# Three token blocks of 768 in place of four of 512 and a rest of 256, with the seven-product up for all of them

## The chip, the cores and the metric

The kernel runs on one core of one Trainium2 chip. The metric is the device time of one execution in microseconds. The profile is of one execution, taken by the hardware profiler; its span runs from the first instruction to the last. Engines: PE is TensorE's matmul stream, PEld its weight loads, DVE is VectorE, ACT ScalarE, POOL GpSimd, SP SyncE, whose queue issues the transfers.

## The reference

Three stages follow each other on 4 x 576 = 2304 tokens. The tokens are tiled by 128 into 18 tiles.

```python
# Performer attention: q, k, v [4, 8, 576, 64], omega [128, 64]
def phi(x):
    proj = np.einsum('bhsd,md->bhsm', x, omega)
    h = proj - np.sum(x * x, axis=-1, keepdims=True) / 2.0
    return np.exp(h - np.max(h, axis=-1, keepdims=True)) / np.sqrt(m)
kv = np.einsum('bhsm,bhsd->bhmd', phi(k_s), v)
num = np.einsum('bhsm,bhmd->bhsd', phi(q_s), kv)       # divided by phi(q) . sum of phi(k)
# dense mixture: x [2304, 512], w1 [8, 512, 1024], w2 [8, 1024, 512]
P = np.exp(x @ w_gate - max)                            # then 8 Sinkhorn steps
for e in range(8):
    out += P[:, e:e + 1] * (np.maximum(x @ w1[e], 0.0) @ w2[e])
# last layer: w_in [512, 2048], w_out [2048, 512], given as float64
h = x @ w_in
out = (h * (1.0 / (1.0 + np.exp(-1.702 * h)))) @ w_out
```

## The kernel before

**Precision.** Each large product runs as float32r passes over exact splits (hi, lo): hi*hi + hi*lo + lo*hi, so each takes three matmuls where one would do. ACT makes hi by a cast, DVE or POOL makes lo by a subtraction.

**Chunks, blocks and visits.** The two layers with hidden columns are cut into chunks of 256 of them: 4 for each of 8 experts and 8 for the last layer, 40 in all. The tokens are four blocks of 512 (one for each batch) and a rest block of 256. A visit is one chunk with one block: an up product, h^T = act(w1^T x^T), and a down product, which adds the chunk's share of y to an accumulator in SBUF (`down`, L877: 6 matmuls of 128x512 for a tile of 128 tokens; the eviction L884 multiplies by the gate and adds; L888 only adds). The up product of a visit is issued ahead of the down product of the visit before it. In expert 0 the visits run block by block while attention gives blocks out, and the chunk order zigzags; from expert 1 on every chunk visits all blocks.

**Two forms of up.** `up` (matmul L714) is the ordinary product. `up_fast` (`prod`, matmul L818) is Winograd's form with seven products of quadrants (half of the chunk's columns, half of the block's tokens), each 6 matmuls of 256 columns. It accumulates in two halves of one PSUM bank `pa` (`le` and `ri`) and in `pc`. The copies L835 and L842 (ACT) and the additions L838, L843 and L847 (DVE) combine them; L689 and L697 make h's hi and lo. It is used for the four blocks of 512 in all chunks but expert 0's, the first of expert 1, called (1,0), and the first of the last layer. The rest block and the other chunks take `up`.

**Weave.** `weave` puts the four down tiles of the visit before between the parts of a fast up: one after the three first products, one after the next two, two after the sixth, and the seventh product last. A visit after the rest block has only two such tiles: none, one, one.

**Weights.** A chunk's w1 is a raw tile from one transfer, split into a pair with two buffers; the sums of quadrants that the fast form takes are made on POOL (L642) and split into another pair (L581). w2 has two rows of 128, each a pair with three buffers. `prepare` says in which visit each is made. The sums of x^T (`x_sums`) are made once for a block.

**Attention and filling.** `attention` steps through the tiles of k and q of each batch. TensorE's work in a query step is `num` (L294), a transpose of x (L342), of the next tile (L202), of features (L287) and the projection `pj` (L227 to L229). After each yield the loop at L1089 takes as much of the mixture's visits as the step's own estimate, once a block of x^T is in `ready`. All general PSUM tiles share one ring of six banks (`ps`). During experts 1 to 7 a background task turns the float64 weights into float32 in 64 pieces (L544 to L566) through a scratch in DRAM.

The order of instructions on each engine is that in which the program issues them (a manual schedule); the generators `moe`, `weave`, `up`, `up_fast`, `down` and the loop at L1089 set it.

## Time and profile before

| | |
|---|---|
| median of 3 runs | 2146.57 us (2145.16 to 2147.8) |
| span of the profiled execution | 2144.3 us |
| PE busy | 2118.2 us, 99%, 13150 matmuls |
| PEld | 1890.2 us, 88% |
| DVE | 1372.2 us, 64% |
| ACT | 741.5 us, 35% |
| POOL | 465.7 us, 22% |

The profiled execution's span is 2.3 us under the median of the timed runs. Matmuls are pipelined: the duration of one (0.28 us at 256 columns) overlaps the next, so the pace is read from the distance between starts. The idle time in a row is that of its engine just before the instruction, with what ended it.

### The profile page before, as it was taken

How to read it: one execution, taken by the hardware profiler on the slowest of the kernel's cores; microseconds unless marked ns; L12 is line 12 of the kernel's file. 1: busy time of each engine (PE TensorE's matmuls, PEld its weight loads, DVE VectorE, ACT ScalarE, POOL GpSimd, SP SyncE). 2: the span in 40 equal slices, each digit the busy share in tenths (PEclk: the TensorE clock that was granted, in tenths of full speed). 3: DMA queues.
4: the chain of work that ended last, by engine and by line, in shares of the span. 5: the costliest groups of instructions: out<-in, count | busy, mean ns of one | idle time of the engine just before them, and what ended most of it. 6: DMA issues, size and time to landing. Idle time of an engine off the chain costs nothing.

```text
span 2144.3 us, 32561 instructions
## 1 busy us (share of the span) xinstructions
PE 2118.2 (99%) x13150; PEld 1890.2 (88%) x13150; DVE 1372.2 (64%) x2625; ACT 741.5 (35%) x1628; POOL 465.7 (22%) x444
## 2 busy tenths in 40 slices
PE   8999999999999999999999999999999999999999
PEld 8888878888989999989899899998998988898888
DVE  7666556676666666666666666666555566655565
ACT  6655442432222222222222222222222245333333
POOL 3222011342211112122111111221111135222320
PEclk9999999999999999999999999999999999999999
DMA  8242111101111111111111111111000000000002
GB/s 184 51 105 58 40 40 40 50 26 45 43 57 42 57 45 50 43 45 43 57 42 49 54 46 47 45 43 52 21 27 23 21 20 21 20 21 20 20 20 89
DMA packets 113383, 97.60 MB, mean 46 GB/s; under 512 B 61008, under 2 KB 90192, under 8 KB 113232
## 3 DMA queue, kind: packets, MB, share of 16 engines
q1 hardware_dynamic: 113232, 95.52, 15.3%
q8 instruction: 103, 1.69, 0.3%
q14 instruction: 48, 0.39, 0.1%
HBM read 82.40 MB, written 13.11 MB: 45 GB/s over the span
## 4 chain that ended last, share of the span: by engine, by line
PE 93%; DVE 4%; ACT 2%; issue 1%; DMA 1%; POOL 0%; SPq 0%; ACTq 0%; DVEq 0%
PE py L877 44%; PE pa L818 27%; PE ph L714 11%; PE pc L818 4%; PE num L294 1%; PE kv L264 1%; DVE w2l L581 1%; PE pj L227 1%; PE pj L229 1%; PE pj L228 1%; DVE mx L231 1%; PE pt L202 1%; ACT feat L247 0%; PE qt L287 0%; DMA r<-in_moe_w_dram 0%
## 5 line engine op out<-in xcount | busy, mean ns | idle before, releaser
L877 PE MATMUL py<-w2h,hh 128*128 128x512 f32 x1440 | 568.6, 395 | 1.7 <-DVE xl L346 0.8
L877 PE MATMUL py<-w2l,hh 128*128 128x512 f32 x1440 | 563.5, 391 | 3.4 <-DVE w2l L581 3.4
L877 PE MATMUL py<-w2h,hl 128*128 128x512 f32 x1440 | 563.2, 391 | 0.6 <-DVE hl L695 0.6
L884 DVE SCALAR_TENSOR_TENSOR a<-py,pg,a 128x512 f32<-128x512 f32 x504 | 374.9, 749 | 162.2 <-PE py L877 153.1
L877 PEld LDWEIGHTS py<-w2h,hl 128*128 128x128 f32 x1440 | 270.3, 188 | 62.1 <-DVE hl L695 1.0
L877 PEld LDWEIGHTS py<-w2l,hh 128*128 128x128 f32 x1440 | 270.7, 188 | 45.9 <-DVE w2l L581 4.7
L877 PEld LDWEIGHTS py<-w2h,hh 128*128 128x128 f32 x1440 | 271.1, 188 | 44.8 <-DVE xl L346 1.0
L818 PE MATMUL pa<-th,w1h 128*128 128x256 f32 x816 | 233.6, 286 | 1.2 <-ACT c L835 0.8
L835 ACT COPY c<-pa 128x512 f32<-128x512 f32 x136 | 79.9, 588 | 444.5 <-PE pa L818 439.5
L818 PE MATMUL pa<-th,w1l 128*128 128x256 f32 x816 | 230.3, 282 | 0.0
L818 PE MATMUL pa<-tl,w1h 128*128 128x256 f32 x816 | 229.0, 281 | 0.0
L566 POOL TENSOR_TENSOR tmp<-tmp 128x256 f32<-128x256 f32 x64 | 47.2, 738 | 777.1 <-DVE tmp L563 409.3
L818 PE MATMUL pa<-xh,w1h 128*128 128x256 f32 x648 | 182.3, 281 | 0.0
L818 PE MATMUL pa<-xh,w1l 128*128 128x256 f32 x648 | 182.2, 281 | 0.0
L818 PE MATMUL pa<-xl,w1h 128*128 128x256 f32 x648 | 181.9, 281 | 0.0
L818 PEld LDWEIGHTS pa<-th,w1h 128*128 128x128 f32 x816 | 153.2, 188 | 18.4 <-ACT c L835 7.3
L689 ACT ACTIVATE hh<-c 128x512 fp32r<-128x512 f32 x216 | 113.5, 526 | 158.0 <-DVE c L847 115.1
L818 PEld LDWEIGHTS pa<-th,w1l 128*128 128x128 f32 x816 | 153.5, 188 | 9.2
L842 ACT COPY c<-pa 128x256 f32<-128x256 f32 x136 | 50.8, 373 | 316.2 <-PE pa L818 316.2
L818 PEld LDWEIGHTS pa<-tl,w1h 128*128 128x128 f32 x816 | 155.5, 191 | 0.0
L843 DVE TENSOR_TENSOR c<-pa,c 128x256 f32<-128x256 f32 x136 | 57.8, 425 | 149.4 <-ACT c L842 149.4
L697 DVE SCALAR_TENSOR_TENSOR hl<-c,hh 128x512 fp32r<-128x512 f32 x216 | 148.2, 686 | 0.0
(183 smaller groups left out, 4137.0 us busy)
## 6 DMA issues: line engine op xcount, KB each, us to landing
r<-in_moe_w_dram SPq DMA_DIRECT2D x82, 512.0 KB, 3.7
raw<-in_moe_w_in_dram SPq DMA_DIRECT2D x32, 256.0 KB, 3.2
raw<-in_moe_w_out_dram SPq DMA_DIRECT2D x32, 256.0 KB, 3.2
k<-in_k_dram SPq DMA_DIRECT2D x16, 256.0 KB, 4.6
v<-in_v_dram SPq DMA_DIRECT2D x16, 256.0 KB, 5.4
q<-in_q_dram SPq DMA_DIRECT2D x16, 256.0 KB, 4.6
scr_in<-tmp SPq DMA_DIRECT2D x32, 128.0 KB, 2.0
scr_out<-tmp SPq DMA_DIRECT2D x32, 128.0 KB, 1.8
```

Source lines behind the costliest of these rows:

```text
L202: nc.tensor.transpose(pt[:, i * P : (i + 1) * P], x[:, 2 * i : 2 * i + 2, :], ident)
L227: nc.tensor.matmul(o, hi[:, p, :], om_hi, start=True, stop=False)
L566: nc.gpsimd.tensor_tensor(out=mf, in0=mf, in1=af, op=ALU.add)
L689: nc.scalar.activation(self.hi, self.src, AF.Relu)
L697: nc.vector.scalar_tensor_tensor(out=self.lo, in0=self.src, scalar=0.0, in1=h, op0=ALU.max, op1=ALU.subtract)
L714: nc.tensor.matmul(ph[:, :n], a[:, kk, fs], x[:, kk, :], start=m == 0, stop=m == 3 * NK - 1)
L818: nc.tensor.matmul(o, a[kk][x], b[kk][y], start=start and kk == 0 and n == 0, stop=kk == 1 and n == 2, skip_group_check=True,)
L835: nc.scalar.copy(s[:, 0:3:2, :], pa.rearrange("p (c n) -> p c n", c=2))
L842: nc.scalar.copy(s[:, 1, :], le)
L843: nc.vector.tensor_tensor(out=s[:, 1, :], in0=ri, in1=s[:, 1, :], op=ALU.add)
L877: nc.tensor.matmul(py, a[:, f, c], w, start=m == 0, stop=m == 3 * NF - 1)
L884: nc.vector.scalar_tensor_tensor(out=o, in0=py, scalar=pg[:, i, e : e + 1], in1=o, op0=ALU.mult, op1=ALU.add)
```

## The change

The tokens become three blocks of six tiles, 768 tokens. `ORDER` places the two tiles that hold the last 64 rows of two batches each behind batches 0 and 1, and behind batches 2 and 3. A quadrant of a block has 384 columns (`Q`). `up_fast` (matmul L817) runs for every block of 35 chunks, all but expert 0's and the first of the last layer; `up` (L705) computes the same quadrants one after the other, 12 matmuls of 384 each. `le` has its own bank twice, `ri` one; the ring `ps` falls from six banks to five. h is kept in quadrants of 384, five buffers for hi and five for lo. The down product is L887, its evictions L894 and L898.

The fast up's parts hold one down tile after the third product, one after the fifth, one after the sixth, and the rest after the seventh.

w1's seven quadrants and sums stand in one raw tile, loaded by four transfers. They are split in three groups (`g0`, `g1`, `g2`) with one buffer each, made new behind the last product of the old chunk that reads the group. w2 is a ring of five tiles: the first hi is made in the middle of a chunk's first visit, the other three (L637, L639) once the last down tile of the chunk before is issued. In attention the inputs are loaded tile by tile, eight steps ahead; logits are taken for half a block; only block 0 is given out before attention ends, and the loop takes 0.65 of the step's estimate.

```diff
     NITER = 8
+    ORDER = [0, 1, 2, 3, 4, 5, 6, 7, 16, 8, 9, 10, 11, 12, 13, 14, 15, 17]
+    PLACE = {i: n for n, i in enumerate(ORDER)}
+    ST = 6
+    NB = NTILE // ST
+    SUP = ST * P
+    Q = SUP // 2
...
-        return ph["sb"].tile(shape, dt, tag="f4", bufs=5, name=name)
+        return ph["sb"].tile(shape, dt, tag="f4", bufs=4, name=name)
 
     def b2(shape, dt, name):
-        return ph["sb"].tile(shape, dt, tag="b2", bufs=15, name=name)
-    def c3(shape, dt, name):
-        return ph["sb"].tile(shape, dt, tag="c3", bufs=1, name=name)
+        return ph["sb"].tile(shape, dt, tag="b2", bufs=26, name=name)
...
+    def sx(name):
+        return big.tile([P, Q], F32, tag="sx", bufs=3, name=name)
...
-        return pp.tile([P, 512], F32, tag="ps", bufs=6, name=name)
+        return pp.tile([P, 512], F32, tag="ps", bufs=5, name=name)
...
+                j, t = divmod(PLACE[token_tile(*seq[s - 3][1:])], ST)
+                if t % 3 == 2:
+                    got = j, t // 3, logits(j, t // 3)
+                    yield 1.39
+                    if t == ST - 1 and j == 0:
+                        ready.add(j)
...
+            if 1 <= s < n - 8:
+                load_tile(*seq[s + 8])
+            if 4 <= s and at(s + 5, "k"):
+                load_tile("v", *seq[s + 5][1:])
...
-    def split_single(r, hi, lo, eng):
+    def split(r, hi, lo, eng):
         nc.scalar.copy(hi, r)
         eng.tensor_tensor(out=lo, in0=r, in1=hi.bitcast(F32), op=ALU.subtract)
 
     class Chunk:
-        """Weights of one chunk as (hi, lo): w1, sums of its quadrants where the up product is the
-        fast one, and w2 in rows of 128."""
+        GROUPS = ((0, 3), (3, 5), (5, 7))
+        SLOT = {(0, 0): 0, (0, 1): 2, (1, 1): 4, (1, 0): 5}
+        T1, T2, T3, T4 = 1, 3, 5, 6
...
-            self.r1 = big.tile([P, NK, FC], F32, tag="r1", name="r1")
-            nc.sync.dma_start(out=self.r1, in_=src)
+            self.raw = big.tile([P, 7, 2, P], F32, tag="w", name="w")
+            for (f, kh), o in self.SLOT.items():
+                nc.sync.dma_start(
+                    out=self.raw[:, o], in_=src[:, 2 * kh : 2 * kh + 2, f * P : (f + 1) * P]
+                )
...
+        def make_sums(self):
+            if self.summed:
+                return
+            self.summed = True
+            r = self.raw
+            for o, x, y in ((1, 5, 0), (3, 4, 1), (5, 4, 5), (6, 2, 3)):
+                nc.gpsimd.tensor_tensor(out=r[:, o], in0=r[:, x], in1=r[:, y], op=ALU.subtract)
+        def split1(self, i, eng):
+            a, b = self.GROUPS[i]
+            pair = [
+                big.tile([P, b - a, 2, P], F32R, tag=f"g{i}{x}", name=f"g{i}{x}") for x in "hl"
             ]
...
+            self.g[i] = pair
+            u = slice(0, b - a) if self.fast else (slice(0, 3, 2), slice(1, 2), slice(0, 1))[i]
+            split(self.raw[:, a:b][:, u], *(x[:, u] for x in pair), eng)
...
+        def split2(self, part):
+            def new():
+                return big.tile([P, DM], F32R, tag="w2", bufs=5, name="w2")
             if part == 0:
...
+                hi = new()
+                nc.scalar.copy(hi, self.r2[:, 0, :])
+                self.w2.append([hi])
+                return
+            for f in range(NF):
+                if f:
+                    self.w2.append([new()])
+                    nc.scalar.copy(self.w2[f][0], self.r2[:, f, :])
+                lo = new()
+                nc.vector.tensor_tensor(
+                    out=lo, in0=self.r2[:, f, :], in1=self.w2[f][0].bitcast(F32), op=ALU.subtract
+                )
+                self.w2[f].append(lo)
...
+    def new_h():
+        return [big.tile([P, Q], F32R, tag=f"h{x}", bufs=5, name=f"h{x}") for x in "hl"]
...
+        le = ph["ps"].tile([P, 512], F32, tag="le", bufs=2, name="le")[:, :Q]
+        ri = ph["ps"].tile([P, 512], F32, tag="ri", name="ri")[:, :Q]
+        pc = ps("pc")[:, :Q]
+        prod(le, 0, b00, True)
         run_late()
...
+        m1 = sx("m1")
+        nc.scalar.copy(m1, le)
+        prod(ri, cur.T1, s1, True)
+        m5 = sx("m5")
+        nc.scalar.copy(m5, ri)
+        prod(pc, 2, b10, True)
+        add(pc, pc, m1)
+        prep("g0")
+        yield 18 * 0.1735
+        yield next(dn)
+        steps(act(0, 0, pc))
+        prod(le, cur.T2, s2, False)
+        u2 = sx("u2")
+        nc.scalar.copy(u2, le)
+        prod(ri, 4, s4, False)
+        add(ri, ri, u2)
+        prep("g1")
+        yield 12 * 0.1735
+        yield next(dn)
+        prod(le, cur.T3, s3, False)
+        add(m5, le, m5)
+        prep("mid")
+        yield 6 * 0.1735
+        yield next(dn)
+        steps(act(0, 1, ri), act(1, 1, m5))
+        prod(le, cur.T4, b11, False)
+        a4 = act(1, 0, le)
+        a4.first()
+        a4.second()
+        prep("g2")
+        yield 6 * 0.1735
+        yield from dn
+        def last():
+            a4.third()
+            a4.last()
+        return h, last
...
-        for t in (2, 3, 0, 1) if cur.fast and j < B else range(ntile(j)):
+        for t in range(ST):
             py = ps("py")
-            c = slice(t * P, (t + 1) * P)
+            th, c = t // 3, slice(t % 3 * P, (t % 3 + 1) * P)
...
+            def prep(at, cur=cur, nx=nx, v=v, left=left):
+                if at == "mid" and v == 0:
+                    cur.split2(0)
+                if not nx:
+                    return
+                if at == "mid" and left == 2:
+                    nx.make_sums()
+                if left == 1 and at[0:1] == "g":
+                    for i in at[1:]:
+                        nx.split1(int(i), nc.gpsimd)
...
+            if v == 0:
+                cur.split2(1)
+                if nx:
+                    nx.load2()
+            if left == 1 and n2:
+                n2.load1()
...
-            credit += dt
+            credit += 0.65 * dt
...
+        ready.update(range(NB))
```

The rest is in words: `x_sums` works on one half of its rows after the other with two scratch buffers; `ffn_in` runs one visit ahead instead of two; the gate `pg` shares the tile of the logits `lg`; `weave` and `prepare` are gone, their work is in `up_fast` and `prep`.

The places in the order of instructions that the prediction speaks of follow. First TensorE where a fast up goes from its third product (`pc`) to its fourth, in before in the visit after the rest block of an expert's chunk (`xh`, `xl` are x^T, `th`, `tl` its sums, `w1h`, `w1l` the weights):

```order
L818 MATMUL pc<-xh_673,w1h 128x256
L818 MATMUL pc<-xh_673,w1l 128x256
L818 MATMUL pc<-xl_674,w1h 128x256
L818 MATMUL pa<-th_4317,w1h 128x256
L818 MATMUL pa<-th_4317,w1l 128x256
L818 MATMUL pa<-tl_4318,w1h 128x256
```

and in after in the first visit of an expert's chunk (`g0h`, `g1h` weight groups, `w_...` tiles of w2):

```order
L817 MATMUL pc<-xh,g0h 128x384
L817 MATMUL pc<-xh,g0l 128x384
L817 MATMUL pc<-xl,g0h 128x384
L887 MATMUL py<-w_11936,hh 128x512
L887 MATMUL py<-w_11997,hh 128x512
L887 MATMUL py<-w_11936,hl 128x512
L887 MATMUL py<-w_11999,hh 128x512
L887 MATMUL py<-w_12001,hh 128x512
L887 MATMUL py<-w_11999,hl 128x512
L817 MATMUL le<-th_3987,g1h 128x384
L817 MATMUL le<-th_3987,g1l 128x384
L817 MATMUL le<-tl_3988,g1h 128x384
```

In before the fourth product follows at once; in after a down tile of six matmuls stands between, and the fourth product goes to `le`.

Second DVE where one chunk's down tiles give way to the next one's. In before (`w2l` is a low of w2, `tmp` a piece of the last layer's weights, `a_...` an accumulator, `hl` a low of h):

```order
L556 SCALAR_TENSOR_TENSOR tmp_6578<-tmp_6578 128x256
L559 TENSOR_SCALAR tmp_6578<-tmp_6578 128x256
L581 TENSOR_TENSOR w2l<-r_6134,w2h 128x512
L697 SCALAR_TENSOR_TENSOR hl<-pa,hh 128x256
L838 TENSOR_TENSOR c<-pc,c 128x256
L563 SCALAR_TENSOR_TENSOR tmp_6578<-raw_6544,tmp_6578 128x256
L884 SCALAR_TENSOR_TENSOR a_1252<-py,pg,a_1252 128x512
L843 TENSOR_TENSOR c<-pa,c 128x256
L884 SCALAR_TENSOR_TENSOR a_1252<-py,pg,a_1252 128x512
```

and in after, where the last eviction of the old chunk stands ahead of both lows of the new chunk's w2:

```order
L535 SCALAR_TENSOR_TENSOR tmp_8981<-tmp_8981 128x256
L538 TENSOR_SCALAR tmp_8981<-tmp_8981 128x256
L894 SCALAR_TENSOR_TENSOR a_4159<-py,lg,a_4159 128x512
L542 SCALAR_TENSOR_TENSOR tmp_8981<-raw_8946,tmp_8981 128x256
L639 TENSOR_TENSOR w_9014<-r_8593,w_8955 128x512
L639 TENSOR_TENSOR w_9018<-r_8593,w_9016 128x512
L678 SCALAR_TENSOR_TENSOR hl<-le,hh 128x384
L828 TENSOR_TENSOR pc<-pc,m_9033 128x384
```

One low stood among the work of the chunk's visits before; now two stand one behind the other, right behind the eviction of the last tile and ahead of the next visit's additions.

Third TensorE in attention where the first ordinary up product is issued. In before, behind the logits of the first block (`kv` is attention's sum, `lp` the logits, `pt` a transpose):

```order
L264 MATMUL kv_878<-v_357,feat 128x65 x8
L357 MATMUL lp<-xh_673,wg 16x512 x4
L361 MATMUL lp<-xl_674,wg 8x512 x4
L202 MATMUL pt<-ident,q_467 128x128 x4
L714 MATMUL ph<-xh_673,w1h 128x512
L714 MATMUL ph<-xh_673,w1l 128x512
L714 MATMUL ph<-xl_674,w1h 128x512
```

and in after:

```order
L289 MATMUL num<-kvs_522,ft 128x65 x8
L327 MATMUL xt<-ident,x 128x128 x4
L342 MATMUL lp<-xh,wg 16x384 x4
L346 MATMUL lp<-xl,wg 8x384 x4
L289 MATMUL num<-kvs_1113,ft 128x65 x8
L705 MATMUL ph<-xh,g0h 128x384
L705 MATMUL ph<-xh,g0l 128x384
L705 MATMUL ph<-xl,g0h 128x384
```

In before four groups of `num` stand ahead of the first up product, in after nine, the ninth's second half right ahead of it.

## Rows read from the trace of the kernel before

**Rows 1.** The page: span, engine totals, and the granted clock in 40 slices.
```profile
span 2144.3 us, 32561 instructions
...
PE 2118.2 (99%) x13150; PEld 1890.2 (88%) x13150; DVE 1372.2 (64%) x2625; ACT 741.5 (35%) x1628; POOL 465.7 (22%) x444
...
PEclk9999999999999999999999999999999999999999
```

**Rows 2.** Windows: busy us (x instructions) by engine, granted clock, DMA share, GB/s.
```profile
0.00:500.00 500.00, 481.51 (x2962) 419.48 (x2963) 321.75 (x596) 231.47 (x568) 123.53 (x103) 1.00 0.26 65
500.00:1700.00 1200.00, 1200.00 (x7530) 1082.19 (x7529) 782.63 (x1533) 330.11 (x679) 221.87 (x238) 1.00 0.14 43
1700.00:2144.00 444.00, 436.73 (x2662) 388.52 (x2660) 267.83 (x497) 179.97 (x381) 120.28 (x103) 1.00 0.09 29
```

**Rows 3.** The page: the chain that ended last, by engine and by line.
```profile
PE 93%; DVE 4%; ACT 2%; issue 1%; DMA 1%; POOL 0%; SPq 0%; ACTq 0%; DVEq 0%
PE py L877 44%; PE pa L818 27%; PE ph L714 11%; PE pc L818 4%; PE num L294 1%; PE kv L264 1%; DVE w2l L581 1%; PE pj L227 1%; PE pj L229 1%; PE pj L228 1%; DVE mx L231 1%; PE pt L202 1%; ACT feat L247 0%; PE qt L287 0%; DMA r<-in_moe_w_dram 0%
```

**Rows 4.** Timeline, TensorE: start us, duration us, line, operands.
```profile
1003.34 0.28 PE L818 MATMUL pa<-xh,w1h 128*128 128x256 f32 x1
...
1006.19 0.39 PE L877 MATMUL py<-w2h,hh 128*128 128x512 f32 x1
...
1014.55 0.28 PE L714 MATMUL ph<-xh,w1h 128*128 128x256 f32 x1
...
1017.43 0.40 PE L877 MATMUL py<-w2h,hh 128*128 128x512 f32 x1
...
1022.90 0.28 PE L818 MATMUL pa<-xh,w1h 128*128 128x256 f32 x1
...
1024.90 0.28 PE L818 MATMUL pc<-xl,w1h 128*128 128x256 f32 x1
1025.15 0.38 PE L818 MATMUL pa<-th,w1h 128*128 128x256 f32 x1
1025.37 0.28 PE L818 MATMUL pa<-th,w1l 128*128 128x256 f32 x1
```

**Rows 5.** Groups by line and shape: busy us, mean ns, idle before.
```profile
L884 DVE SCALAR_TENSOR_TENSOR a<-py,pg,a 128x512 f32<-128x512 f32 x504 | 374.9, 749 | 162.2 <-PE py L877 153.1
...
L581 POOL TENSOR_TENSOR w1l<-s,w1h 128x512 fp32r<-128x512 f32 x68 | 86.6, 1292 | 59.8 <-ACT w1h L580 59.8
...
L835 ACT COPY c<-pa 128x512 f32<-128x512 f32 x136 | 79.9, 588 | 444.5 <-PE pa L818 439.5 <-DVE hl L697 3.7 <-DVE pa L683 1.0
...
L247 ACT ACTIVATE feat<-pj,nb 128x128 f32<-128x128 f32 x272 | 74.2, 387 | 76.9 <-DVE nb L243 67.8 <-PE py L877 8.7
...
L581 DVE TENSOR_TENSOR w2l<-r,w2h 128x512 fp32r<-128x512 f32 x62 | 62.3, 1006 | 48.4 <-ACT w2h L580 47.9
...
L580 ACT CAST w2h<-r 128x512 fp32r<-128x512 f32 x98 | 60.8, 621 | 1.2 <-PE py L877 1.1
...
L556 DVE SCALAR_TENSOR_TENSOR tmp<-tmp 128x256 f32<-128x256 uint32 x64 | 26.8, 418 | 0.0
...
L559 DVE TENSOR_SCALAR tmp<-tmp 128x256 uint32<-128x256 uint32 x64 | 18.8, 294 | 2.2
```

**Rows 6.** Line L581 alone: duration ns as min/median/max.
```profile
L581 DVE TENSOR_TENSOR w2l<-r,w2h x62: 677/687/2517, 80.6 to 2099.0; 128x512 fp32r<-128x512 f32 x62
```

**Rows 7.** Timeline, TensorE in attention: start, duration, idle before and releaser.
```profile
34.04 0.39 PE L227 MATMUL pj<-om_hi,xh 128*128 128x256 f32 x1 [0.86 <-ACT feat L247]
...
36.53 2.00 PE L294 MATMUL num<-kvs,ft 128*128 128x65 f32 x16 [0.49 <-ACT ft L288]
...
50.20 0.66 PE L287 MATMUL qt<-ident,feat 128*128 128x128 f32 x4 [0.50 <-DVE xl L211]
...
68.42 0.48 PE L714 MATMUL ph<-xh,w1h 128*128 128x512 f32 x1
```

More of the change, by code (lines that the diff above doesn't have):

```diff
@@ L119, in setup @@
         make_identity(nc, ident)
-        load_main(0, "k")
+        for t in range(NT):
+            load_tile("k", 0, t)
         nc.gpsimd.memset(ones, 1.0)
@@ L846, in up_fast, with act @@
-        prod(le, sa[2], t3, False)
-        nc.vector.tensor_tensor(out=s[:, 2, :], in0=le, in1=s[:, 2, :], op=ALU.add)
-        a1.second()
-        a1.third()
-        a2.first()
-        a1.last()
-        a2.second()
-        a2.third()
-        yield 6 * 0.109
-        a2.last()
-        prod(le, a22, t4, False)
-        a3.first()
-        a3.second()
-        late.extend((a3.third, a3.last))
-        yield 6 * 0.109
-        return hh, hl
+        def act(th, f, src):
+            h[th, f] = hi, lo = new_h()
+            return Act(e, src, hi, lo, sx("g") if e == E else None)
@@ L949, in background @@
             run(spare)
-        elif urgent and not paused[0]:
+        elif urgent:
             run(urgent)
@@ L1037, in moe @@
+            if nx and left == 1:
+                nx.make_sums()
+            dn = down(*pend) if pend else iter(())
             if ch == (1, 0):
-                apply_gate(j)
-            if cur.fast and j < B:
+                dn = gated_down(dn, j)
+            if cur.fast:
                 while (ch[0] // E, j) not in sums_done:
+                    while begun():
+                        run(spare)
                     run(urgent)
-                h = yield from weave(up_fast(cur, j), down(*pend), ntile(pend[1]))
+                h, last = yield from up_fast(cur, j, dn, prep)
@@ L1043, in moe @@
             else:
-                h = yield from up(cur, j, lambda: prepare(cur, nx, n2, v, left, "between"))
-                if pend is not None:
-                    yield from down(*pend)
+                h, last = yield from up(cur, j, dn, prep)
             key = (ch[0] // E, j)
-            first = key not in seen
+            pend = (cur, j, h, key not in seen, ch == chunks[-1].ch)
             seen.add(key)
-            pend = (cur, j, h, first, ch == chunks[-1].ch)
-            prepare(cur, nx, n2, v, left, "after")
```

496 lines of the change are left out of this document (180 added, 316 removed).

## The prediction

> **What bounds the kernel now.** I read the page's engine totals first, then the stretches, the chain, TensorE's own timeline, and last the groups of the other engines. TensorE is busy for 2118.2 us of a span of 2144.3 at a granted clock in the top tenth, VectorE for 64% and ScalarE for 35% [rows 1]. By stretches TensorE's idle time lies at the two ends: 18.5 us of the first 500, none of the 1200 from 500 to 1700, 7.3 us of the last 444, all at granted clock 1.00, that is 2.4 GHz [rows 2]. The chain gives 93% to TensorE, nearly all of that to the down product L877 and the up product L818 [rows 3]. So the kernel lasts as long as TensorE's list of products, plus what the start loses. A change helps by shortening that list, and hurts where it makes TensorE wait.
>
> The list is priced by start-to-start intervals, since the durations of pipelined matmuls overlap [rows 4]. Fast products of 256 columns: 24 from 1003.34 to 1006.19, 0.1188 us each. Ordinary ones of 256 columns: 24 from 1014.55 to 1017.43, 0.120. Of 512 columns: 24 from 1017.43 to 1022.90, 0.228, and a little more elsewhere; I use 0.229. One fast chunk of before is 168 + 24 + 108 of these: 19.96 + 2.88 + 24.73 = 47.57 us. The middle stretch has 7530 matmuls in 1200 us, or 47.81 us for 300 [rows 2]. The missing 0.24 us is visible once a chunk: behind the last pc product at 1024.90 the next starts at 1025.15 and the one after at 1025.37, 0.25 and 0.22 instead of 0.119 each [rows 4]. There the visit of the 256-token rest leaves no down tile between pc and the next write of pa, which must wait for the copy L835.
>
> **The change part by part.**
>
> *Fast visits.* All 40 chunks keep 18 down tiles of 6 matmuls, so L877 costs what it did. A fast chunk's up product goes from 168 + 24 matmuls of 256 columns to 3 x 42 = 126 of 384. No row has 384 columns. The straight line between 0.1188 (256) and 0.229 (512) gives 0.1739, which I take because it lies between measured sizes. The bounds are proportions: 0.229 x 384/512 = 0.1718 below, 0.1188 x 384/256 = 0.1782 above. 126 x 0.1739 = 21.91 against 22.84 us: -0.93 in each of 34 chunks, **-31.6**.
>
> *Chunk (1,0) becomes fast.* Before: 4 x 24 x 0.229 + 24 x 0.120 = 24.86; after: 21.91. **-2.95**.
>
> *Five chunks stay ordinary* (expert 0's four and the first of the last layer): 144 x 0.1739 = 25.04 against 24.86, **+0.9** together.
>
> *The wait once a chunk.* In after a down tile of 6 x 0.229 = 1.37 us always stands between pc and the next write of le, and le has two buffers; that is the first pair of fences of the change. 34 x 0.232 = **-7.9**. If something else is late in its place this is worth nothing (bound 0).
>
> *What is late next in a steady visit.* A product of 6 lasts 1.04 us and a tile 1.37, so a visit is 7 x 1.04 + 6 x 1.37 = 15.5 us. I walked it with the rows' durations. The copies of le and ri cost under the 0.588 of L835 and have two products' time. The add into pc runs under the first tile. The weight groups have one buffer, but each is re-split behind the last product of the chunk that reads it: a cast (0.621 for 512 wide) and a POOL subtraction (1.292) [rows 5], 1.9 us against 9 or more until the next chunk reads the group. Cost nothing; if that cover went it would be part of the 1.9 us per chunk. VectorE has six evictions at 0.749, and four lows and three adds of 384 columns that I put at no more than an eviction of 512 each: under 9.8 us of 15.5, so it stays off the path on average.
>
> *The exchange of w2* is the tight place; the second pair of fences shows it. Only hi0 can be made early, since five buffers hold four tiles of the old chunk. After the chunk's last down tile VectorE has its eviction (0.749), at most one step of a piece of the last layer's weights (0.418 and 0.294: 0.71), and the two lows L639. The next chunk's first tile starts three products later, at 3.13 us, and needs the last low four matmuls on: 3.13 + 0.92 = 4.05. With lows at the median 0.687 [rows 6] the chain is 0.75 + 0.71 + 1.37 = 2.83, with lows at the mean 1.006 [rows 5] 3.47. Slack 0.6 to 1.2 us: cost nothing. In expert 0 the first tile stands behind 12 matmuls only, 2.09 us, and the slack is a few tenths; I count that in the next term.
>
> *Attention.* An ordinary product can fill TensorE there only when a block is ready. The first L714 is at 68.42 us, behind four num groups of query tiles; in after the first L705 stands behind nine (third pair of fences). In unfilled steps TensorE waits 0.86 us for an exponential, 0.49 for the copied features and 0.50 for a projection's low [rows 7]; at some 0.6 a step five more cost 3. The ring of general PSUM buffers falls from six to five, so a projection must wait for the exponentials of the step before (four of 0.387, 1.55 us for half a step [rows 5]); I count 3, with 0 and about 12 (eight steps at 1.55) as ends. VectorE has, by a count of its instructions and the durations of their like, an estimated 18 us of work in expert-0 visits of 16.6 where Sinkhorn steps, lows and x_sums meet: two visits, 2 to 3. Together **+8**, from 0 (filler reaches the lost time anyway) to +20.
>
> Sum: -31.6 - 2.95 + 0.9 - 7.9 + 8 = -33.5. Against the profiled 2144.3 that is 2110.8. The median of the runs is 2146.57, 2.3 us above the profile's span, so the forecast is **2113 us**.
>
> On TensorE's fixed cost a rule speaks against the first term. The rows give 0.1188 and 0.229 for 256 and 512 columns, so 8.6 ns of each matmul do not go with the columns, and this is what fewer, wider products save. The Trainium skill, "TensorE: Matmul & The Clock Gate", section "Wait — 56ns, not 53.3ns?", puts a warm matmul at N / 2.4 GHz plus about 2.5 ns. By it a fast chunk's up product would go from 192 x 0.1092 = 20.97 to 126 x 0.1625 = 20.48 us, -0.49 instead of -0.93, and the sum would end near 2127 (an estimate from that page). This case's rows differ from it, 0.1188 and not 0.1092, and the measurement decides; as a result of its own it lies between the forecast and rival C, and its chance is in C's.
>
> **The rivals.**
>
> A, slower: the w2 exchange waits at each of 46 weight exchanges (36 chunks and ten in expert 0's zigzag). For it: the low L581 has a median of 687 ns but a maximum of 2517 and a mean of 1006 [rows 5, 6], so some instances take over 2 us, and in after all 92 lows run on VectorE while POOL re-splits weights. With one low at 2.52 and one at 1.01 the chain is 0.75 + 0.71 + 1.01 + 2.52 = 4.99, 0.94 late; 46 x 0.94 = 43 us: 2156. It makes the change slower once the chain passes 4.05 + 33.5/46 = 4.8 us. Against it: in most instances the low takes 0.69, and POOL's re-split of the last group should end about 2 us before the exchange. The Trainium skill, "SBUF — State Buffer", section "Who interferes with whom", says that a VectorE operation with two SBUF inputs contends with a GpSimd one that reads SBUF, and that the loser blocks for the whole instruction. The spread of L581 agrees with that.
>
> B, attention loses its filler: the five-buffer ring stalls most unfilled steps, and VectorE's load in expert 0 delays the first tile of its visits. That ends at 2113 + 12 to 20, about 2129. For it: the first 500 us hold 18.5 of TensorE's 26 idle us. Against: with a filler the steps of before keep TensorE busy.
>
> C, wider products do not save their fixed part: 384 columns at 0.1782. 35 x 126 + 5 x 144 = 5130 matmuls x 0.0043 = +22: 2135. The other bound, 0.1718, gives 5130 x -0.0021 = -11: 2102. Against both: two measured sizes and a clock that does not move.
>
> D, nothing is gained: the steady wait stays in another place (+8), attention costs +20 and the widths are at C's half (+11): 2113 + 31 = 2144, beside the time of before.
>
> **How the numbers follow.** The forecast, 2103 to 2123: 0.71. B: 0.11. C: 0.06, half of it on the low side. D: 0.04. A: 0.08. What this kernel's runs can tell from no change is 0.2%, 4.3 us. Faster by more holds the forecast, B and C, 0.88, less 0.01 for sums of their bad ends: 0.87. Same takes D and that 0.01: 0.05. Slower is A: 0.08. The range leaves out A's upper part and the farthest low end: 2096 to 2143.
>
> **What would show it.** In the profile of the changed kernel: L817 and L705 with intervals of 0.172 to 0.178 us; some 10700 matmuls in place of 13150, and steady stretches with TensorE at 100%; a fast chunk of three visits in 46.6 us; no interval over 0.3 us behind pc. A shows as TensorE waiting for L639 at chunk changes, with L639 well above 0.69. B shows as idle time in the first 300 us of more than 30 us. The prediction is wrong if a fast visit lasts longer than 15.9 us, or if any group of waits in the steady part passes 10 us in total.

## The result: slower by 0.7%

The changed kernel takes 2160.85 us (2159.99 to 2162.35), the kernel before 2147.19 beside it: ratio 1.0066, interval 1.0052 to 1.008. The profiled execution has a span of 2158.7 us, 14.4 more than before, where the sum said 33.5 less.

The page of the changed kernel, span, totals and granted clock:

```profile
span 2158.7 us, 29072 instructions
...
PE 2111.3 (98%) x11040; PEld 1900.3 (88%) x11040; DVE 1367.2 (63%) x2525; ACT 750.8 (35%) x1635; POOL 465.9 (22%) x475
...
PEclk9999999999999999999999999999999999999999
```

TensorE is still the bound, with 2110 matmuls fewer and only 6.9 us less busy time than in [rows 1]. The same stretches as in [rows 2], in the same columns:

```profile
0.00:500.00 500.00, 468.57 (x2879) 422.31 (x2880) 306.67 (x621) 228.87 (x596) 128.82 (x149) 0.99 0.26 60
500.00:1700.00 1200.00, 1199.65 (x5955) 1081.89 (x5954) 768.29 (x1401) 340.46 (x664) 241.78 (x238) 1.00 0.14 43
1700.00:2158.00 458.00, 443.08 (x2209) 396.08 (x2208) 292.19 (x503) 181.42 (x377) 95.34 (x88) 1.00 0.09 28
```

Idle time went from 18.5 to 31.4 us at the start and from 7.3 to 14.9 at the end; the middle has none. Where the time went is read from the start of chunk (1,1), the last matmul of the experts' last fast product, the starts of the second and third chunk of the last layer, and the last matmul. In before and then in after (start, duration):

```profile
446.47 0.28 PE L818 MATMUL pa<-xh,w1h 128*128 128x256 f32 x1
...
1733.88 0.28 PE L818 MATMUL pa<-xl,w1h 128*128 128x256 f32 x1
...
1798.66 0.28 PE L818 MATMUL pa<-yh,w1h 128*128 128x256 f32 x1
...
1849.27 0.28 PE L818 MATMUL pa<-yh,w1h 128*128 128x256 f32 x1
...
2139.24 0.39 PE L877 MATMUL py<-w2h,hl 128*128 128x512 f32 x1
```

```profile
468.97 0.33 PE L817 MATMUL le<-xh,g0h 128*128 128x384 f32 x1
...
1740.91 0.34 PE L817 MATMUL le<-xl,g2h 128*128 128x384 f32 x1
...
1808.76 0.33 PE L817 MATMUL le<-yh,g0h 128*128 128x384 f32 x1
...
1862.86 0.33 PE L817 MATMUL le<-yh,g0h 128*128 128x384 f32 x1
...
2153.51 0.39 PE L887 MATMUL py<-w,hl 128*128 128x512 f32 x1
```

| stretch | before | after | difference | at equal work | by the sum |
|---|---|---|---|---|---|
| to chunk (1,1): attention, expert 0, (1,0) | 446.5 | 469.0 | +22.5 | +28.0 | +5.8 |
| 27 chunks of the experts | 1287.4 | 1271.9 | -15.5 | -21.0 | -31.3 |
| last layer | 405.4 | 412.6 | +7.2 | +7.2 | -7.9 |

(By the sum: +8 - 2.95 + 0.7; 27 x -1.16; 7 x -1.16 + 0.2.) When chunk (1,1) starts, two down tiles of the chunk before it are still to come in before, but six in after. Four tiles are 24 matmuls, 5.5 us; "at equal work" moves them into the first stretch. At the second boundary the work left agrees within 1 us. So the stretches miss the sum by 22, 10 and 15 us, and the main cause differs from one to the next.

### The profile page after: what moved, and what is told of

Its sections match the earlier page's. It is cut to its first block, busy times and chain, and to the rows that moved or that the text cites. A ratio compares the mean times of both kernels' runs of the same rounds, so it can differ in the third digit from the quotient of the medians.

```text
span 2158.7 us, 29072 instructions
## 1 busy us (share of the span) xinstructions
PE 2111.3 (98%) x11040; PEld 1900.3 (88%) x11040; DVE 1367.2 (63%) x2525; ACT 750.8 (35%) x1635; POOL 465.9 (22%) x475
## 3 DMA queue, kind: packets, MB, share of 16 engines
q1 hardware_dynamic: 139664, 92.38, 15.5%
## 4 chain that ended last, share of the span: by engine, by line
PE 89%; DVE 6%; POOL 2%; ACT 2%; issue 1%; DMA 0%; SPq 0%; ACTq 0%; POOLq 0%; DVEq 0%
PE py L887 43%; PE le L817 20%; PE ri L817 10%; PE pc L817 5%; PE ph L705 4%; POOL u L756 2%; PE num L289 2%; PE kv L259 1%; DVE t L756 1%; PE pj L225 1%; PE pj L227 1%; PE pj L226 1%; DVE tl L759 1%; DVE mx L229 1%; ACT feat L245 0%
## 5 line engine op out<-in xcount | busy, mean ns | idle before, releaser
L887 PE MATMUL py<-w,hh 128*128 128x512 f32 x2880 | 900.9, 394 | 12.4 <-ACT feat L245 4.9
L887 PEld LDWEIGHTS py<-w,hh 128*128 128x128 f32 x2880 | 535.7, 189 | 101.1 <-ACT feat L245 5.4
L887 PE MATMUL py<-w,hl 128*128 128x512 f32 x1440 | 570.5, 396 | 4.1 <-DVE hl L678 3.7
L894 DVE SCALAR_TENSOR_TENSOR a<-py,lg,a 128x512 f32<-128x512 f32 x504 | 377.9, 751 | 269.4 <-PE py L887 264.7
L887 PEld LDWEIGHTS py<-w,hl 128*128 128x128 f32 x1440 | 271.4, 188 | 63.3 <-DVE hl L678 4.9
L560 POOL TENSOR_TENSOR g0l<-w,g0h 128x768 fp32r<-128x768 f32 (+1 forms) x46 | 79.2, 1722 | 662.3 <-ACT g0h L559 662.3
L607 POOL TENSOR_TENSOR w<-w 128x256 f32<-128x256 f32 x140 | 110.1, 807 | 68.8 <-DMA w<-in_moe_w_dram 46.0
L898 DVE TENSOR_TENSOR o<-py,o 128x512 f32<-128x512 f32 x126 | 85.7, 690 | 59.6 <-PE py L887 59.6
L828 DVE TENSOR_TENSOR ri<-ri,u 128x384 f32<-128x384 f32 x105 | 59.2, 564 | 64.2 <-PE ri L817 22.9
L245 ACT ACTIVATE feat<-pj,nb 128x128 f32<-128x128 f32 x272 | 73.9, 382 | 68.8 <-DVE nb L241 65.2
L836 ACT COPY m<-le 128x384 f32<-128x384 f32 x105 | 50.3, 479 | 125.2 <-PE le L817 125.2
L637 ACT CAST w<-r 128x512 fp32r<-128x512 f32 x46 | 28.7, 624 | 137.9 <-PE py L887 137.9
L817 PE MATMUL le<-th,g2h 128*128 128x384 f32 x210 | 71.8, 342 | 1.5 <-ACT u L848 1.3
```

The lines of the kernel that those rows point to most:

```text
L245: nc.scalar.activation(f[:, h, :], pvs[h // 4][:, h % 4, :], AF.Exp, bias=nb[:, h : h + 1])
L560: eng.tensor_tensor(out=lo, in0=r, in1=hi.bitcast(F32), op=ALU.subtract)
L607: nc.gpsimd.tensor_tensor(out=r[:, o], in0=r[:, x], in1=r[:, y], op=ALU.subtract)
L817: nc.tensor.matmul(o, a[kk][x], b[kk][y], start=start and kk == 0 and n == 0, stop=kk == 1 and n == 2, skip_group_check=True,)
L828: nc.vector.tensor_tensor(out=o, in0=a, in1=b, op=ALU.add)
L887: nc.tensor.matmul(py, a[:, c], w, start=m == 0, stop=m == 3 * NF - 1)
```

## The experiments

All times are medians of timed runs; each ratio is against the kernel before on the same chip.

### Attention: banks of PSUM, or the late first block

A PSUM bank of the ring comes free when the last engine that reads its tile is done. In after the longest waits in attention are at tiles that need a free bank, as in these rows of TensorE's timeline (start, duration, idle before and releaser), L245 being the exponentials:

```profile
179.74 0.45 PE L705 MATMUL ph<-xh,g0h 128*128 128x384 f32 x1 [2.44 <-ACT feat L245]
...
189.07 1.22 PE L887 MATMUL py<-w,hh 128*128 128x512 f32 x2 [2.44 <-ACT feat L245]
...
201.37 0.73 PE L887 MATMUL py<-w,hh 128*128 128x512 f32 x2 [2.44 <-ACT feat L245]
```

**e4**, five banks in the kernel before:

```diff
-        return pp.tile([P, 512], F32, tag="ps", bufs=6, name=name)
+        return pp.tile([P, 512], F32, tag="ps", bufs=5, name=name)
```

> The kernel before with the general ring of PSUM at five banks instead of six, nothing else. Theory of the ring: attention loses 6 to 12 us by waits for L247, 2153 to 2159. Rival, the late first block: with filler from 68 us on, five banks cost under 3 us, 2146 to 2150.

2173.33 us, 1.012 (1.0105 to 1.0135): 26 us for one bank, more than any theory gave. Chunk (1,1) starts at 471.66 instead of 446.47. The longest waits are not for the exponentials L247, as the theory had it, but for lows L346, which read a transpose of x out of its bank (total us, times, longest):

```profile
PE py L877 <- DVE xl L346: 7.2, 3, 2.6
```

The granted clock (third number from the end) is lower too, here from 100 to 200 us:

```profile
100.00:200.00 100.00, 95.16 (x567) 83.30 (x566) 55.06 (x103) 45.74 (x124) 15.05 (x13) 0.91 0.37 82
```

In the three slices of 100 us that follow it is 0.95, 0.99 and 0.98; in before it is 1.00 in all four. What is missing adds up to 17 us, so by an estimate from these rows up to 17 of the 26 us are slower matmuls, and not the waits themselves.

**e8**, the late block alone, in the kernel before with its six banks:

```diff
-                    ready.add(j)
+                    if j:
+                        ready.add(j)
+                if seq[s - 3] == ("q", 1, 1):
+                    ready.add(0)
```

> The kernel before with its first block of x^T given to the up products only when the second query tile of batch 1 has its logits, as the six-tile block comes in the changed kernel; six banks and all else as before. Theory of the late block: attention's unfilled steps cost 6 to 12 us, 2153 to 2159. Rival, the ring alone: with six banks the unfilled steps cost no more than 4 us, 2147 to 2151.

2159.34 us, 1.0061 (1.0044 to 1.0077): 12 us, at the upper end of that theory. So either costs time by itself in the kernel before.

**e5**, six banks in the changed kernel; the ninth bank that this would need in the later phase is taken from le, which attention does not use:

```diff
-        return pp.tile([P, 512], F32, tag="ps", bufs=5, name=name)
+        return pp.tile([P, 512], F32, tag="ps", bufs=6, name=name)
-        le = ph["ps"].tile([P, 512], F32, tag="le", bufs=2, name="le")[:, :Q]
+        le = ph["ps"].tile([P, 512], F32, tag="le", bufs=1, name="le")[:, :Q]
```

> The changed kernel with six banks in the general ring of PSUM and one for le instead of two; nothing else. Theory of the ring: five banks cost 26 us in the kernel before, so here too attention and the first visits get most of it back, 15 to 25 us faster than the changed kernel, 2136 to 2146. Rival, the late first block: the idle time of attention is there because no up product can be given before 110 us, and only the three waits of 2.44 us and a little more go: 3 to 8 us faster, 2153 to 2158. A single le should cost nothing in steady visits, since three down tiles stand between its last product and its next first one.

2424.01 us, 1.129 (1.1275 to 1.1308): the total was far off, and the part in question is read from the trace. The first fast product, in after and then in e5:

```profile
418.75 0.33 PE L817 MATMUL le<-xh,g0h 128*128 128x384 f32 x1
...
395.88 0.33 PE L817 MATMUL le<-xh,g0h 128*128 128x384 f32 x1
```

It comes 22.9 us earlier. From 100 to 200 us, in after and then in e5:

```profile
100.00:200.00 100.00, 90.80 (x627) 81.60 (x626) 56.86 (x115) 52.40 (x151) 15.64 (x20) 0.98 0.28 60
```

```profile
100.00:200.00 100.00, 98.70 (x709) 92.24 (x708) 60.54 (x121) 55.54 (x162) 18.94 (x23) 1.00 0.26 56
```

82 more matmuls in the same 100 us, and no wait for L245 is left in them. With its 50.2 us for chunk (1,0) as in after, chunk (1,1) would start at 446.1; at equal work (5.5 us) that is 5.1 later than before, where the sum had 5.8, 3 of it for the ring. So the ring explains nearly all that the first stretch misses. Of the late block no loss beyond the sum is left to see, for chunk (1,0) itself, in which the experts' sums of x^T are made, takes 3.1 us more than the 47.1 of a steady chunk. Most of what e5 lost is at the single le (e5, all waits of TensorE for two lines):

```profile
PE le L817 <- DVE hl L678: 162.7, 82, 5.6
PE le L817 <- DVE hl L676: 42.1, 20, 6.7
```

The seventh product's activation is issued behind the next visit's first product, and with one le that product must wait for it.

**e2, e9, e13**: three ways to give attention the eighth bank and leave le alone: to the transposes pt; to the second half of pj; or two rings, four banks and two.

```diff
-        pt = ps("pt")                       # e2
+        pt = pst("pt")
-            pj = ps("pj")                   # e9
+            pj = pst("pj") if half else ps("pj")
-            o = ps("ph")[:, :Q]             # e13, pc likewise; ps: 4 in attention, 3 after it
+            o = psu("ph")[:, :Q]
```

> The changed kernel with attention's transposes of q and k (L200, pt) in a PSUM bank of their own, the eighth that attention leaves free, so that the ring of five is left to the other tiles. Theory of the ring (attention is slow because a tile must wait until the exponentials of the step before give a bank back): the three waits of 2.44 us for L245 and most of the shorter ones at L200 go, and the low clock behind them: 8 to 13 us faster than the changed kernel, 2148 to 2153. Rival, the late first block (TensorE has no up product until 110 us, 68 before, and the unfilled steps wait for the chain of copies and lows, not for a bank): at most 3 us faster, 2158 to 2161.

> The changed kernel with the second half of each projection in attention (pj, which the exponentials hold longest) in the eighth bank of PSUM, which attention leaves free; le keeps its two banks. Theory of the ring, corrected after the variants before (six banks brought the first fast product 23 us earlier, and only the single le, whose last activation is issued behind the next visit's first product, lost it again): 15 to 23 us faster than the changed kernel, 2138 to 2146. Rival, one bank that a single kind of tile may use serialises like the one for pt did: no gain, 2158 to 2170.

> The changed kernel with the general PSUM tiles in two rings: two banks for the accumulators of the ordinary up (ph) and the third product (pc), and four in attention, three after it, for all others; le keeps its two banks. So attention has six banks with nothing else changed. Theory of the ring: the first fast product starts 15 to 23 us earlier, 2138 to 2146. Rival, the late first block carries the loss in attention: at most 6 us, 2155 to 2161.

2176.96 us (1.0141, 1.0126 to 1.0156), 2155.75 (1.0039, 1.0024 to 1.0054) and 2177.14 (1.0136, 1.0119 to 1.0152). e2 and e13 were misses: slower than the changed kernel by 16 us. Only the bank for half of pj gained, 5 us. In e2 TensorE waits 13.7 us at the transposes L200 for the lows L209 and 15.5 more there with no releaser that the profile shows, which fits tiles that wait for each other at their one bank. Why e13 lost is not settled. The reason that e9 was expected to gain, that the exponentials hold pj longest, is not what the trace shows. In after a pj tile keeps its bank for 4.5 us on average in attention, from its first matmul to the end of its last reader; a transpose of q or k keeps it for 6.6 us and one of x for 7.4, as here, where its low stands far back in VectorE's queue:

```profile
171.61 0.66 PE L327 MATMUL xt<-ident,x 128*128 128x128 f32 x4
...
181.86 0.68 DVE L331 TENSOR_TENSOR xl<-xt,xh 128x512 fp32r<-128x512 f32 x1
```

No run here moved these lows ahead.

### The pace of 384 columns

From the start of one chunk to that of the next in the steady part, 1412.77 to 1459.89, after takes 47.12 us (234 matmuls): 0.69 less than the 47.81 of before, where the sum had 46.64. Of the 47.12, 126 intervals of L817 are 22.26 (0.1766 each; the sum had 21.91) and 108 of the tiles L887 are 24.86 (24.73). The intervals depend on what ran before. The seventh product of a visit in after, behind a down tile, with the first matmul of the tile that follows:

```profile
1407.58 0.33 PE L817 MATMUL le<-xh,g2h 128*128 128x384 f32 x1
1407.75 0.34 PE L817 MATMUL le<-xh,g2l 128*128 128x384 f32 x1
1407.93 0.34 PE L817 MATMUL le<-xl,g2h 128*128 128x384 f32 x1
1408.11 0.35 PE L817 MATMUL le<-xh,g2h 128*128 128x384 f32 x1
1408.29 0.34 PE L817 MATMUL le<-xh,g2l 128*128 128x384 f32 x1
1408.47 0.34 PE L817 MATMUL le<-xl,g2h 128*128 128x384 f32 x1
1408.65 0.63 PE L887 MATMUL py<-w,hh 128*128 128x512 f32 x2
```

Six in 1.07 us. In e1 (below) seven products run in one stretch of 42, which begins with the seventh of one visit; the rows are the first matmuls of that product, of the next visit's first three, and of the tile behind the stretch:

```profile
1410.73 0.33 PE L817 MATMUL le<-xh,g2h 128*128 128x384 f32 x1
...
1411.79 0.33 PE L817 MATMUL le<-xh,g0h 128*128 128x384 f32 x1
...
1412.83 0.34 PE L817 MATMUL ri<-th,g0h 128*128 128x384 f32 x1
...
1413.89 0.34 PE L817 MATMUL pc<-xh,g0h 128*128 128x384 f32 x1
...
1418.11 0.62 PE L884 MATMUL py<-w,hh 128*128 128x512 f32 x2
```

The first product, with no tile ahead, takes 1.04, the 0.1739 of the forecast; behind a tile in after it takes 1.07. The second, a product of sums, takes 1.06 with no tile ahead. All 42 take 7.38, 0.1757 each. Three kernels change how often the streams alternate. **e1**: all six tiles between the sixth and the seventh product. **e6**: three there and three behind the seventh; the second sum's copy ahead of the first activation. **e15**: one tile behind each product from the second on.

```diff
-        yield next(dn)                      # e1: both places, and the one after T3
         steps(act(0, 0, pc))
...
         steps(act(0, 1, ri), act(1, 1, m5))
+        yield from dn
         prod(le, cur.T4, b11, False)
```

> The changed kernel with the six down tiles of a fast visit in one stretch between the sixth and the seventh product, instead of one, one, one and three: seven products then run in one stretch of 42, with one stretch of six tiles. Theory of the switches (each passage between the 384-column up stream and the 512-column down stream costs some 0.025 us, since the first six matmuls behind one start 0.171, 0.175, 0.178, 0.185, 0.176, 0.182 us apart and later ones 0.1735): two passages a visit instead of eight, 0.15 to 0.16 us less in each of 105 fast visits, 16 to 17 us faster than the changed kernel, near 2144; mean interval of L817 0.1742 and of L887 0.2276. Rival, the pace belongs to a product's operands: L817 stays at 0.1767 and the time within 3 us of 2160.9. Second rival, the tiles were needed to hide the combining copies: slower by 0.5 us a visit, over 2200.

> The changed kernel with three down tiles between the sixth and the seventh product and three behind the seventh, and the copy of the second sum ahead of the first activation on ScalarE: four passages between the streams a visit instead of eight, and always three tiles in front of a product that waits for a combining copy. Theory of the switches: 0.08 to 0.10 us less in each of 105 fast visits, and none of the waits for L847 that the variant with one stretch had in the last layer: 2150 to 2153, a chunk in 46.8 to 46.9 us. Rival: the pace does not depend on the passages, the chunk stays at 47.1 and the time at 2159 to 2162.

> The changed kernel with one down tile behind the second, third, fourth, fifth, sixth and seventh product: twelve passages between the streams a visit instead of eight. Theory of the switches (2 passages 46.76, 4 passages 46.96, 8 passages 47.12 us a chunk, so 0.02 us a passage and visit): 47.36 us a chunk, 6 to 10 us slower than the changed kernel in the steady part. Rival, the slower chunk belongs to where a product waits for a combining copy: more tiles between cover it, and the chunk is 47.1 or less.

| passages a visit | 2 (e1) | 4 (e6) | 8 (after) | 12 (e15) |
|---|---|---|---|---|
| us a chunk, steady | 46.76 | 46.96 | 47.12 | 47.24 |
| of it 126 of 384 columns | 22.14 | 22.22 | 22.26 | 22.24 |
| of it 108 of 512 columns | 24.62 | 24.74 | 24.86 | 25.00 |
| total, us | 2180.34 | 2166.06 | 2160.85 | 2167.89 |

(e1's 46.76 holds in the last nine expert chunks; the others take 47.0, and in the last layer 49.5.) The chunk goes with the passages, by less than forecast: 0.36 for e1 against 0.47, and 0.12 for e15 against 0.24. Most of it is in the tiles, 0.24 of the 0.36; the products gain 0.12 and stay 0.23 above the sum's 21.91, which borders on the rival: part of the pace belongs to the product. The totals of e1 and e6 were misses (ratios 1.0153 and 1.0089, each within 0.0015), for tiles also hide the combining copies; e15's (1.0092) is 7 us above the changed kernel, close to its forecast. In e1 TensorE waits 17.2 us for the second sum's copy, which stands behind an activation in ScalarE's queue:

```profile
PE le L817 <- ACT u L847: 17.2, 21, 2.5
```

In e6 that is cured, and 11.3 us of waits for the first copy L836 are left, where ScalarE waits at a cast of x_sums for POOL's sums (3.29 us once) with the copy behind it. The tiles between products that the forecast took for free cost 0.01 to 0.03 us a passage.

### The first chunks of the last layer

**e3**: POOL's part of x_sums on VectorE.

```diff
-        def tt(out, a, b, op, eng=nc.gpsimd):
+        def tt(out, a, b, op, eng=nc.vector):
```

> The changed kernel with all additions of the block sums of x^T on VectorE, where seven of ten a half were on POOL. Theory of the queue (in the first visits of the last layer a cast on ScalarE waits for POOL's sums, with the sigmoid and the high part of h behind it, and TensorE waits 3.5 us): that wait goes and the first visits of the last layer lose 4 to 7 us less; 2154 to 2157. Rival, VectorE is the crowded engine there: the sums of seven more operations of 0.55 us a half push its lows back, and the time is the same or up to 6 us longer, 2161 to 2167.

2165.63 us, 1.0082 (1.0065 to 1.0099): the rival's number, but not its place. Most of the loss is ahead of the last layer: the first fast product starts at 430.67 instead of 418.75. From the start of the experts' last chunk to that of the last layer's second, e3 takes 110.3 us and after 113.3, so the theory's wait does get shorter by 3 us; the chunk after it, 54.1 us long in after, takes 54.35. **e17** leaves the last layer's sums out; its products take zeros for them.

```diff
+        if key[0]:
+            nc.gpsimd.memset(th.bitcast(F32), 0.0)
+            nc.gpsimd.memset(tl.bitcast(F32), 0.0)
+            sums_done.add(key)
+            yield
+            return
```

> The changed kernel with the sums of x^T of the last layer left out: their tiles are set to zero and the block's own columns stay as they are, so the last layer's products take wrong operands of the same shape. Theory: the sums' chain over POOL, VectorE and ScalarE delays the first two chunks of the last layer; without it the second chunk falls from 54.1 to 47.2 us and the first from 67.8 to about 64: 9 to 11 us less, 2150 to 2152. Rival, the delay is the passage from experts to last layer (transposes of y, the new activation chain): the chunks stay within 2 us, 2158 to 2161.

2148.95 us, 1.0004 (0.9994 to 1.0013): 12 us. From the last expert product on, the same boundaries as above:

```profile
1743.04 0.34 PE L823 MATMUL le<-xl,g2h 128*128 128x384 f32 x1
...
1804.04 0.33 PE L823 MATMUL le<-yh,g0h 128*128 128x384 f32 x1
...
1851.16 0.33 PE L823 MATMUL le<-yh,g0h 128*128 128x384 f32 x1
```

61.0 and 47.1 us instead of 67.9 and 54.1. So the sums cost 14 us in these two chunks. The kernel before pays for them as well, some 3 us: its second chunk of the last layer takes 50.6 us, where a steady one takes 47.8. The forecast had the difference of 11 us for nothing. The longest of the waits can be followed in after. POOL makes sums of weights (L607) between two sums of x^T, a cast of ScalarE (L793) waits for the second, and the high part of h (L668) that TensorE needs stands behind that cast:

```profile
1785.68 3.19 POOL L607 TENSOR_TENSOR w<-w 128x256 f32<-128x256 f32 x4
...
1790.95 0.51 ACT L793 CAST yh<-u 128x384 fp32r<-128x384 f32 x1 [3.08 <-POOL u L756]
...
1792.69 0.50 ACT L668 CAST hh<-ph 128x384 fp32r<-128x384 f32 x1
...
1793.25 1.22 PE L887 MATMUL py<-w,hh 128*128 128x512 f32 x2 [3.49 <-ACT hh L668]
```

e3, with the sums off POOL, has no wait of that length there. Which queue carries the rest is not settled: VectorE is then the fuller one, and moving the casts (e14 below) gained 0.9 us in the second chunk and lost as much ahead of it.

### Versions

**e7** is e5 with e6's order and sums on VectorE in the last layer, **e10** e5 with the seventh product's activation issued at once, **e11** e10 with the sums on VectorE, **e12** e9 with one stretch as in e1 (the copy first) and the sums, **e14** e12 with the casts of the last layer's x_sums on POOL, **e16** e14 with e13's two rings instead of the pj bank.

> Six banks in the ring, three and three tiles, and the sums of x^T on VectorE in the last layer alone. If ring, switches and queue are three separate costs they add up: 2161 - 20 - 10 - 4 = 2127, between 2122 and 2136, faster than the kernel before. If the late first block is the main cost: 2140 to 2146.

> Six banks in the ring, one for le, and the activation of the seventh product issued right behind that product instead of behind the next visit's first one. Theory: with the activation early the single le is free 1.4 us before the next visit writes it, a chunk is back at 47.1 us, and the ring's gain of 23 us stays: 2136 to 2142. Rival, a single le waits in any order: a chunk above 49 us, over 2200.

> The variant with six banks and the early activation, with the sums of x^T of the last layer on VectorE. Theory of the queue: 2 to 5 us less than without, 2132 to 2139. Rival: VectorE is as late as POOL was, no difference beyond 1.5 us.

> The changed kernel with the second pj half in the eighth bank, all six tiles in one stretch ahead of the seventh product (the copy of the second sum now ahead of the first activation on ScalarE), and the last layer's sums on VectorE. Theory of the switches: the chunk of 46.76 us of the first variant with one stretch, 0.36 under the changed kernel, in 35 chunks, 12 us, with the ring's 15 to 23 and 2 to 5 of the sums: 2121 to 2133. If the combining copies are exposed behind x_sums' casts at the start of each layer, as 14 us were in the variant with three and three tiles: 2135 to 2145.

> The variant with the pj bank, one stretch of tiles and the last layer's sums on VectorE, with x_sums' casts of the last layer on POOL instead of ScalarE. Theory of the queue: the second chunk of the last layer, 58.1 us there against 46.8 for the later ones, falls to 47 to 50 us, so 8 to 11 us less: 2134 to 2138. Rival, POOL is slower still and TensorE waits for the sums themselves: 58 us or more, 2143 to 2155.

> Six banks as four and two, one stretch of tiles, sums on VectorE and casts on POOL in the last layer. If the three costs are separate they add: 2161 - 18 (banks) - 12 (stretch) - 10 (first chunks of the last layer) = 2121, between 2116 and 2130, some 1.2% faster than the kernel before. If the banks do no more than the pj bank did: 2132 to 2137.

| | e7 | e10 | e11 | e12 | e14 | e16 |
|---|---|---|---|---|---|---|
| us | 2487.51 | 2210.73 | 2205.98 | 2145.11 | 2144.89 | 2372.09 |
| ratio | 1.1588 | 1.0291 | 1.0271 | 0.9990 | 0.9986 | 1.1036 |

(Intervals within 0.002.) A single le waits in any order tried (e10: 48.8 us a chunk). In e16, with three banks for tiles and six tiles in a row, TensorE waits 136.6 us for evictions of the experts. e14 fails its theory: the second chunk of the last layer is at 57.2 us against 58.1. Of the other forecasts, e7's and e16's were missed; e10 ended near its rival, e11 is 5 us under e10 as its theory has it, and e12 is at the slow end of its second case.

**e18** has six shared banks, le in turn from its own bank and from the ring, one stretch and the sums on VectorE in the last layer:

```diff
-        le = ph["ps"].tile([P, 512], F32, tag="le", bufs=2, name="le")[:, :Q]
+        odd[0] = not odd[0]
+        le = (ps("le") if odd[0] else ph["ps"].tile([P, 512], F32, tag="le", name="le"))[:, :Q]
```

> Six shared banks in the ring, le in turn from its own bank and from the ring, so that two visits in a row never share it; one stretch of tiles; the last layer's sums on VectorE. Theory: the first fast product comes at 393 us as with six banks before, against 411 with the pj bank, and a chunk stays at 46.76: 2145 - 18 = 2127, between 2122 and 2131, faster than the kernel before by 0.8 to 1.1%. Rival, le in the ring makes tiles wait: a chunk of 47.2 or more, 2140 or more.

2125.45 us, 0.9893 (0.9875 to 0.9912), near its 2127: faster than both kernels. The first fast product starts at 397.21, a chunk takes 46.76, so the ring's and the passages' gains add up; the second chunk of the last layer still takes 56.4. Its stretches, to set beside those of after:

```profile
0.00:500.00 500.00, 482.56 (x2986) 440.92 (x2987) 319.14 (x648) 235.14 (x610) 133.81 (x153) 0.99 0.27 62
500.00:1700.00 1200.00, 1200.00 (x6016) 1088.25 (x6015) 752.23 (x1407) 338.17 (x671) 235.51 (x234) 1.00 0.15 42
```

## Why the prediction was wrong

- *Attention* is the step that failed most: "The ring of general PSUM buffers falls from six to five ... I count 3, with 0 and about 12 as ends". The ring costs 23 us (e5), 26 in the kernel before (e4). The bound counted half a step's exponentials in eight unfilled steps. The filled steps wait as well, because their up products and tiles take banks from the same ring; the lows of transposes hold banks longer than the exponentials do; and a lower granted clock comes with the waits. Rival B named the mechanism and priced it at 12 to 20 us more than the sum; 20 more is what came.
- *Bound and fast visits.* Right that TensorE bounds and that fewer, wider matmuls shorten its list. The interval was taken as 0.1739 from two measured sizes; it is 0.1766 in the woven order and 0.1757 with hardly a passage (e1). The tiles that should cost what they did take 0.13 us a chunk more than the sum. With the wait that goes, a chunk gains 0.69 us, not 1.16: 16 us in 34 chunks, half of the term "fast visits". Rival C named this and went further, to 0.1782.
- *Not in the sum:* the sums of x^T of the last layer, 14 us, 11 more than before (e17). Why three blocks pay more than four was not tested. 20, 16 and 11 make 47 of the 47.9 us by which the profiled span misses the sum.
- *The wait once a chunk* of [rows 4] is gone. In four chunks of the experts another of 0.35 us came (47.47 us instead of 47.12), at the seventh product of the last visit, behind the tile that should cover its addition: 1.4 us in all.
- *The exchange of w2*, rival A, did not come: L639 averages 0.761 us with a maximum of 1.502, and TensorE waits for it 3.5 us in all. In before all 14 lows L581 on VectorE that take over 1.4 us overlap an instruction of POOL; in after 22 of the 92 lows L639 overlap one, and a single one takes that long.
- *The signs.* A steady visit takes 15.7 us (15.9 was the limit), and TensorE is idle for 27.9 of the first 300 us (over 30 would have shown B). They watched waits in the steady part and idle time, and so missed a slower pace, a lower clock and the two ends. "Some 10700 matmuls" was miscounted: the sum's own terms give 11032, and 11040 ran.
- The three causes all push the same way, and the sum had 3 us for one of them and nothing for the others. Rival D, which added three costs, had 0.04.

## What to carry to other kernels

Change the size of a shared ring of PSUM banks by itself and measure it, before anything else that is to pay for it: one bank was worth 23 to 26 us here, and a bank kept for one kind of tile did not replace it. Look at which reader holds each bank longest, and not only at the one that ended the wait. A pace put between two measured sizes was low by 1.6% here, and the order of the streams moved it too; price short pieces by rows of short pieces. Work that is made once a layer, like block sums, belongs in the sum with the visits in which it must be done. And when the parts of a result are read between two boundaries, the work left at each boundary must be the same in both kernels.

## What the runs showed of the hardware

At granted clock 1.00 six matmuls of 384 columns take from 1.04 to 1.07 us, the same for a given product in every steady visit. The first product of a visit takes 1.07 behind three tiles of 512 columns (after, e6), 1.04 with none ahead (e1), and 1.04 behind a single tile (e15). Products of sums take 1.06 either way. So the passage from 512 columns is one condition and not the only one; why is open.

Second, the granted clock fell to 1.2 GHz behind idle stretches in attention (TensorE busy for 2.52 and 2.63 us of the two stretches of 4 us ahead; granted clock is the third number from the end):

```profile
196.00:200.00 4.00, 2.52 (x16) 1.94 (x16) 3.49 (x8) 1.07 (x2) 0.00 (x0) 1.00 0.00 0
200.00:204.00 4.00, 2.63 (x11) 2.31 (x12) 0.76 (x3) 2.55 (x9) 0.00 (x0) 0.83 0.01 4
204.00:208.00 4.00, 4.00 (x18) 4.00 (x18) 2.25 (x4) 0.00 (x0) 0.00 (x0) 0.50 0.00 0
```

In before no slice of 100 us in attention is under 1.00; in after the slices from 100 to 400 us have 0.98, 0.97 and 0.98, and in e5 1.00, 0.97 and 1.00. What is missing is 7 us and 3 us, so by an estimate from these rows up to 4 of the 23 us that the ring costs in the changed kernel are the clock.
